# A two-layer attention and MLP kernel: a priority table and new durations for its planner, LayerNorm in tile pairs, PSUM cleared by matmuls, Q and K weights in halves

## The chip, the cores and the metric

One core of one Trainium2 chip. The metric is device time in microseconds (us), the median of several executions. In the profile PE is the engine for matrix multiplication (PEld its weight load), DVE the vector engine, ACT the engine for activation functions, POOL the GpSimd engine, SP the engine that issues the DMA copies. PSUM is the memory that PE writes its results to; an eviction is a copy from there to SBUF, by ACT or DVE. "Granted clock" is the share of full TensorE clock that the records show.

## The reference

A block of sliding-window attention (32 heads of 16, window 256) and an MLP with GELU, both behind a LayerNorm, applied twice to 2048 rows of 512, with the same weights both times.

```python
def _A_ref(x, wqkv, wo):                       # H = 32, Dh = 16, W = 256
    q, k, v = ...                              # x @ wqkv, split by heads
    scores = einsum("bhqd,bhkd->bhqk", q, k) * Dh ** -0.5
    mask = (i - j >= 0) & (i - j < W)
    o = einsum("bhqk,bhkd->bhqd", softmax(where(mask, scores, -1e9)), v)
    return o.reshape(B, S, D) @ wo
def _B_ref(x, w1, b1, w2, b2):                 # D = 512, F = 1792
    return gelu(x @ w1 + b1) @ w2 + b2
x = A_x
x = x + _A_ref(_layernorm(x)); x = x + _B_ref(_layernorm(x))
x = x + _A_ref(_layernorm(x)); x = x + _B_ref(_layernorm(x))
```

## The kernel before

The kernel is a list of operations with a small planner. `add` records an operation: its engine, an assumed duration, what it reads and writes, a priority, perhaps a second engine that could do it ("place"). `run` plays the engines forward in assumed time. Each free engine takes the ready operation with the lowest priority number. The resulting order becomes the engines' queues. The program gives each engine its queue in that order, with semaphore waits for what an operation needs. So a plan made with wrong durations is still correct, but its queues may put an operation that is not ready in front of one that is.

```python
class _Plan:
    OVER = {"pe": 0.0, "act": 105.0, "dve": 82.0, ...}   # engine is free this much before the result
    LAT = {..., "act": {"pe": 57.0, "act": 60.0, "dve": 34.0, ...}, ...}
    def add(self, eng, fn, dur, reads, writes, prio, alloc, free, ..., alt): ...
    def run(self): ...                                    # list scheduling, smallest prio first
# ... cut ...
for h in range(2):                                        # PSUM cleared by DVE
    add("dve", lambda e, B, h=h: e.memset(ps[:, 4*h : 4*h+4, :], 0.0), 2200, ...)
# ... cut: X, then Wqkv in three whole parts, Wo, W1, W2, b2, b1 are loaded by SP ...
def layernorm(tau, layer, dst, dcol, dname, prio):        # one tile of 128 rows
    add("dve", bn_stats ...); add("dve", bn_aggr ...)
    add("pool", veps = var + EPS, 215, ...)               # 128 x 1
    add("pool", rstd = veps ** -0.5, 590, ...)            # 128 x 1
    add("dve", xn = (X - mean) * rstd, 310, ...)
    add("pe", transposes ...); evac(...)                  # xn -> PSUM -> xnT
def visit(g):                                             # 160 visits: 512 score columns, 4 PSUM banks
    add("pe", scores of both halves -> 4 banks)
    for half in 0, 1:                                     # the second is ordered after the first
        add("act", exp of 2 banks -> E, 1025, ...)
# ... mask(u): E *= mask on DVE or POOL; pv(c): probabilities times V, which reads Va and Vs,
#     Vs being V shifted by half a tile, copied Va -> Vs by DMA; outproj; mlp ...
```

The softmax here doesn't subtract the row's maximum and nothing guards it: scores larger than these inputs give would overflow.

Of the kernel before, what the change touches and what calls it, by code (L numbers as in the profile page):

```python
# [6 lines left out]
dt = mybir.dt  # L7
# [159 lines left out]

class _Plan:
# [7 lines left out]
        "act": {"pe": 57.0, "act": 60.0, "dve": 34.0, "pool": 78.0, "sp": 75.0},  # L176
# [7 lines left out]
    def __init__(self, pools):  # L184
        self.nodes = []
        self.lw = {}
        self.lr = {}
        self.pools = pools
        self.affinity = 0.0

    def add(self, eng, fn, dur, reads=(), writes=(), prio=0.0, alloc=None, free=(), after=(), geo=None,
            table=None, dma=False, alt=(), war=(), lock=False):
        i = len(self.nodes)
        deps = set(after)
# [13 lines left out]
        if free and eng == "dve":  # L208
# [4 lines left out]
            alts=((eng, fn, dur, 0.0, lock),) + tuple(alt), done=False,  # L213
# [144 lines left out]
def bass_interleave_layers__sliding_block__dense_activation_gelu__prompt_kernel(  # L358
# [13 lines left out]
    P = 128  # L372
# [30 lines left out]
    GLAG = 26  # L403
# [3 lines left out]
    POOL_M = 1175.0  # L407
# [7 lines left out]
    JOBS = [(0, 2), (2, 2), (4, 4), (8, 4), (12, 4), (16, 4), (20, 4), (24, 4), (28, 2), (30, 2)]  # L415

# [9 lines left out]
    with ExitStack() as kctx:  # L426
        S_ = _Sched(nc, kctx)

        def sb(name, shape, dtype=dt.bfloat16):
# [13 lines left out]
        veps = sb("veps", [P, 2 * NT], dt.float32)  # L443
        mhalf = sb("mhalf", [P, 1], dt.float32)
# [25 lines left out]
        })  # L470
# [3 lines left out]
        add("pool", lambda e, B: e.memset(ident[:], 1.0), 150, writes=["ident"])  # L474
        add("pool", lambda e, B: e.affine_select(
            ident[:], ident[:], [[-1, P]], ALU.is_ge, 0.0, base=0, channel_multiplier=1), 300,
            reads=["ident"], writes=["ident"])
        add("pool", lambda e, B: e.affine_select(
            ident[:], ident[:], [[1, P]], ALU.is_ge, 0.0, base=0, channel_multiplier=-1), 300,
            reads=["ident"], writes=["ident"])  # L480
        add("pool", lambda e, B: e.memset(mhalf[:], -0.5), 100, writes=["mhalf"])
        add("pool", lambda e, B: e.memset(parmask[:], 0.0), 100, writes=["parmask"])
        for par in range(2):
            for i in range(HC):
                add("pool", lambda e, B, i=i, par=par: e.affine_select(
                    parmask[:, par : par + 1], parmask[:, par : par + 1], [[0, 1]], ALU.is_ge,
                    1.0 if i % 2 == par else 0.0, base=Dh * i - 1, channel_multiplier=-1), 190,
                    reads=["parmask"], writes=["parmask"])
        add("pool", lambda e, B: e.memset(mask01[:], 1.0), 150, writes=["mask01"])

        for i, conds in enumerate((((1, 0, -1),), ((1, HK, -1), (0, -HK, 1)))):
            for st, base, cm in conds:
                add("pool", lambda e, B, i=i, st=st, base=base, cm=cm: e.affine_select(
                    mask01[:, i, :], mask01[:, i, :], [[st, HK]], ALU.is_ge, 0.0, base=base, channel_multiplier=cm), 250,
                    reads=["mask01"], writes=["mask01"])
        add("pool", lambda e, B: e.tensor_tensor(out=mask01[:, 0, :], in0=mask01[:, 0, :], in1=mask01[:, 1, :], op=ALU.add), 300,
            reads=["mask01"], writes=["mask01"])
        add("pool", lambda e, B: e.tensor_scalar(
            out=mask01[:, 1, :], in0=mask01[:, 0, :], scalar1=-1.0, scalar2=1.0, op0=ALU.mult, op1=ALU.add), 300,
            reads=["mask01"], writes=["mask01"])  # L500
        add("pool", lambda e, B: e.memset(Va[:, :, :, Dh:VW], 1.0), 600, writes=["V%d" % i for i in range(VR)])

        for h in range(2):
            add("dve", lambda e, B, h=h: e.memset(ps[:, 4 * h : 4 * h + 4, :], 0.0), 2200, writes=["ps:init%d" % h], prio=-200)

        def dma(fn, writes, reads=(), dur=2200.0, prio=0.0, issue=330.0):
            add("sp", fn, dur, reads=reads, writes=writes, prio=prio, dma=True, geo=issue)
# [6 lines left out]
        load_x(0, 2, -100, 3900.0)  # L514
        load_x(2, 2, -99.5, 4700.0)
        for which in range(3):
            dma(lambda e, B, which=which: e.dma_start(
                Wqkv_sb[:, :, which * D : (which + 1) * D],
                A_wqkv[:, which * D : (which + 1) * D].rearrange("(c p) n -> p c n", p=P)),
                ["Wqkv%d" % which], prio=-99 + which, dur=6500.0 + 1700 * which)  # L520
        load_x(4, 4, -96, 11000.0)
        dma(lambda e, B: e.dma_start(Wo_sb[:], A_wo.rearrange("(c p) n -> p c n", p=P)), ["Wo"], prio=-95, dur=6000.0)
        load_x(8, 8, -94, 14000.0)
# [12 lines left out]
        def evac(dst, src, n, reads, writes, prio, free=(), after=(), two=False, kind="", boot=False):  # L536

            return add("dve", lambda e, B: e.tensor_copy(dst(B), src(B)), 410 if two else d_psum(n),
                       reads=reads, writes=writes + ([] if free else reads), prio=prio, free=free, after=after,
                       alt=() if kind not in ACT_OK and not boot else (("act", lambda e, B: e.activation(dst(B), src(B), AF.Copy, scale=1.0), d_act(n), 0.0 if boot else ACT_H, False),))  # L540
# [3 lines left out]
        def layernorm(tau, layer, dst, dcol, dname, prio):  # L544

            t = tau % T
            k = 2 * tau + layer
            s = xn_rr[0] % NXN
            xn_rr[0] += 1
            k6 = xn_rr[0] % 8  # L550
            add("dve", lambda e, B: e.bn_stats(stat6[:, k6, :], X[:, t, :]), 680,  # L551
                reads=["X%d" % t], writes=["st%d" % k6], prio=prio)
            add("dve", lambda e, B: e.bn_aggr(statmv[:, k, :], stat6[:, k6, :]), 150,
                reads=["st%d" % k6], writes=["mv%d" % k], prio=prio)
            add("pool", lambda e, B: e.tensor_scalar(
                out=veps[:, k : k + 1], in0=statmv[:, k, 1:2], scalar1=EPS, scalar2=None, op0=ALU.add), 215,
                reads=["mv%d" % k], writes=["ve%d" % k], prio=prio - 500, lock=True)
            add("pool", lambda e, B: e.tensor_tensor(  # L558
                out=rstd[:, k : k + 1], in0=veps[:, k : k + 1], in1=mhalf[:], op=ALU.pow), 590,
                reads=["ve%d" % k, "mhalf"], writes=["rs%d" % k], prio=prio - 500, lock=True)  # L560
            add("dve", lambda e, B: e.tensor_scalar(  # L561
                out=xn[:, s, :], in0=X[:, t, :], scalar1=statmv[:, k, 0:1], scalar2=rstd[:, k : k + 1],
                op0=ALU.subtract, op1=ALU.mult), 310,
                reads=["X%d" % t, "mv%d" % k, "rs%d" % k], writes=["xn%d" % s], prio=prio, lock=True)
            g = "tp%d" % k

            def tr(e, B):
                for c in range(DC):
# [4 lines left out]
                alloc=("o", [(g, 1)]), geo="f", war=[dname])  # L573
            evac(lambda B: dst[:, :, dcol : dcol + P],
                 lambda B: psb[:, B[g][0], 0 : DC * P].rearrange("p (c q) -> p c q", c=DC), 512,
                 ["ps:" + g], [dname], prio, free=[g], two=True, kind="t", boot=True)

        def pe_group(g, mms, dur, step, reads, prio, cls="o", after=(), fresh=True, war=()):

            for i in range(0, len(mms), step):  # L580
                part = mms[i : i + step]

                def fn(e, B, part=part):
# [6 lines left out]
                    alloc=(cls, [(g, 1)]) if (i == 0 and fresh) else None, geo="f", after=after, war=war)  # L590

        def residual(tau, layer, g, prio):
            t = tau % T
            add("dve", lambda e, B: e.tensor_tensor(out=X[:, t, :], in0=X[:, t, :], in1=ps[:, B[g][0], :], op=ALU.add),  # L594
                d_psum(512), reads=["X%d" % t, "ps:" + g], writes=["X%d" % t], prio=prio, free=[g])

        def lnq(b, prio):

            xs = b % 2
            for j in range(2):  # L600
                layernorm(2 * b + j, 0, xnTA[:, xs], j * P, "xa%d_%d" % (xs, j), prio)
            xr = ["xa%d_0" % xs, "xa%d_1" % xs]
            cols = [b % QR] + ([QR] if b % QR == 0 and b % RB else [])
            for i in range(DC // 2):
# [3 lines left out]
                for n, cb in enumerate(cols):  # L608
# [4 lines left out]
                        free=[g] if n == len(cols) - 1 else (), after=prev, kind="q", boot=b < 2),)  # L613

        def proj(g, which, i, xs, xr, prio, war):
            for half in range(2):
# [3 lines left out]
                         256, 2, xr + ["Wqkv%d" % which], prio, fresh=(half == 0), war=war)  # L620

        def kv(b, prio, vprio):
# [3 lines left out]
            for i in range(DC // 2):  # L626
# [8 lines left out]
                    prio=prio, free=[g])  # L635
            for j in range(2):
# [3 lines left out]
                              dc == 0, dc == DC - 1) for dc in range(DC)], 512, 1, xr + ["Wqkv2"], vprio, war=["V%d" % (tau % VR)])  # L640
                evac(lambda B, tau=tau: Va[:, tau % VR, :, 0:Dh],
                     lambda B, g=g: ps[:, B[g][0], :].rearrange("p (h d) -> p h d", d=Dh), 512,
                     ["ps:" + g], ["V%d" % (tau % VR)], vprio, free=[g], kind="v", boot=b < 1)
# [15 lines left out]
        def attention(b, prio):  # L659
# [11 lines left out]
            def visit(g):  # L671
# [13 lines left out]
                def sc(e, B):  # L685
# [12 lines left out]
                    writes=["ps:" + gA, "ps:" + gB], prio=pv, alloc=("sc", [(gA, 2), (gB, 2)]), geo="r")  # L698
                aft = (gelu_last[0],) if gelu_last[0] is not None else ()
                a = ()  # L700
                for gi, g_ in enumerate((gA, gB)):
                    if gi == 1:
# [4 lines left out]
                        table="exp", after=a + aft),)  # L707
                last_exp[0] = a[0]

            def mask(u, n):  # L710
# [4 lines left out]
                add("dve", lambda e, B: e.tensor_tensor(out=Ew, in0=Ew, in1=Mw, op=ALU.mult), 355 * n,  # L715
                    reads=["E%d%s" % (es, x) for es in ess for x in "ab"] + ["mask01"], writes=["E%dd" % es for es in ess],
                    prio=prio + 10 * u, lock=True,
                    alt=(("pool", lambda e, B: e.tensor_tensor(out=Ew, in0=Ew, in1=Mw, op=ALU.mult), POOL_M * n, POOL_H, True),))  # L718

            def pv(c):  # L720
# [9 lines left out]
                def fn(e, B):  # L730
# [15 lines left out]
                add("pe", fn, 600.0, reads=rd, writes=["ps:" + g], prio=pr, alloc=("od", [(g, 2)]), geo="c", war=["OD%d" % s])  # L746
                add("dve", lambda e, B: e.transpose(OD[:, s, :], ps[:, B[g][0] : B[g][0] + 2, 0 : 2 * P]), 715,  # L747
                    reads=["ps:" + g], writes=["OD%d" % s], prio=pr, free=[g])
                sums = OD[:, s, :].rearrange("p (a k n) -> p a k n", a=2, n=32)
                add("dve", lambda e, B: e.reciprocal(Rc[:, s, :].rearrange("p (a k) -> p a k", a=2), sums[:, :, :, Dh]), 205,  # L750
                    reads=["OD%d" % s], writes=["Rc%d" % s], prio=pr - 800)

                def norm(e, B):
# [4 lines left out]
                add("dve", norm, 360, reads=["OD%d" % s, "Rc%d" % s], writes=["N%d" % s], prio=pr - 700, lock=True,  # L758
                    alt=(("pool", norm, 741, 0.0, True),))
                add("dve", lambda e, B: e.transpose(OT[:, bs, c, :], Nb[:, s, :]), 420,  # L760
                    reads=["N%d" % s], writes=["OT%d_%d" % (bs, c)], prio=pr - 600)
# [14 lines left out]
            for j in range(2):  # L776
                outproj(2 * b + j, pr + 10 * j)

# [129 lines left out]
```

## Time and profile before

Median 537.6 us in three runs (534.4 to 539.3); the profiled run has a span of 535.7 us. First the page's busy times (busy us, share of the span, instructions), then, over 40 equal slices, PE's busy tenths and the granted clock in tenths, and at last the engines of the chain that ended last (followed back from the last instruction, at each step to what released it):

```profile
PE 472.1 (88%) x8944; PEld 254.8 (48%) x8944; DVE 387.3 (72%) x739; ACT 427.4 (80%) x514; POOL 292.4 (55%) x376
...
PE   3886688998979999599999879998999879989997
...
PEclk9997979999979999689999999999999989999999
...
PE 60%; DVE 18%; ACT 18%; issue 2%; POOL 2%; POOLq 0%; DVEq 0%
```

PE has 63.6 us without work and ACT 108. The table of waits (engine, line, tile, what it waited for: us, times, longest) has this pair near its head, among waits of DVE and POOL:

```profile
ACT E L704 <- PE ps L691: 58.1, 46, 4.4
...
PEld ps L691 <- ACT E L704: 33.5, 70, 1.6
```

Exponentials wait for scores, and scores wait for exponentials to free PSUM: neither engine is full, they miss each other. Next is the start, from the timeline (start, length, engine, line, operation):

```profile
1.29 1.76 DVE L504 MEMSET ps<- 128x2048 f32 x1 [1.29 <-PEq L893]
...
3.43 1.76 DVE L504 MEMSET ps<- 128x2048 f32 x1 [0.38 <-issue]
...
5.11 1.22 DVE L551 BATCH_NORM_STATS2 stat<-X 128x6 f32<-128x512 bf16 x2
...
8.31 0.61 PE L569 MATMUL ps<-ident,xn 128*128 128x128 bf16 x4 [8.31 <-DVE xn L561]
...
10.47 3.19 PE L585 MATMUL ps<-xnTA,Wqkv_sb 128*128 128x256 bf16 x16 [0.69 <-ACT xnTA L540]
...
20.64 1.94 ACT L704 ACTIVATE E<-ps 128x1024 bf16<-128x1024 f32 x2
```

### The profile page before, as it was taken

What the parts mean: (1) busy time and instruction counts of PE and PEld (TensorE: products, weight loads), DVE (VectorE), ACT (ScalarE), POOL (GpSimd) and SP (SyncE); (2) the same over time, 40 slices, a digit from 0 to 9 for tenths busy, and PEclk for the clock granted to TensorE, in tenths of its full rate; (3) what the DMA queues carried; (4) which work ended last, traced back from release to release, by engine and by line L of the source; (5) the groups of instructions that cost most, each with busy time, mean ns of one, the idle gap of its engine ahead of it and who ended that gap; (6) DMA issues with size and microseconds to landing.
All of it is one profiled execution on the core that took longest, in us unless ns stands there. A gap on an engine that the chain in (4) does not pass through costs nothing.

```text
span 535.7 us, 19845 instructions
## 1 busy us (share of the span) xinstructions
PE 472.1 (88%) x8944; PEld 254.8 (48%) x8944; DVE 387.3 (72%) x739; ACT 427.4 (80%) x514; POOL 292.4 (55%) x376
## 2 busy tenths in 40 slices
PE   3886688998979999599999879998999879989997
PEld 2543455555544545345444444444544444444563
DVE  5996878496979578775899588884878648793531
ACT  2689779888987988979888988689876888699552
POOL 6576746274684457452588347860585425871410
PEclk9997979999979999689999999999999989999999
DMA  8910001010100001000000011000110001100000
GB/s 277 325 42 23 2 4 23 1 25 1 24 2 13 12 3 23 4 1 22 14 13 3 2 23 23 2 4 6 33 29 21 2 8 39 42 2 4 29 21 29
DMA packets 16020, 15.82 MB, mean 30 GB/s; under 512 B 3264, under 2 KB 15424, under 8 KB 15936
## 3 DMA queue, kind: packets, MB, share of 16 engines
q1 hardware_dynamic: 15936, 14.56, 9.5%
q8 instruction: 70, 1.15, 0.9%
q14 instruction: 14, 0.11, 0.1%
HBM read 8.00 MB, written 2.10 MB: 19 GB/s over the span
## 4 chain that ended last, share of the span: by engine, by line
PE 60%; DVE 18%; ACT 18%; issue 2%; POOL 2%; POOLq 0%; DVEq 0%
PE ps L585 46%; ACT E L704 12%; PE ps L737 6%; PE ps L691 6%; DVE KT L629 3%; DVE xn L561 2%; DVE stat L551 2%; ACT gT L820 2%; DVE E L715 2%; PE ps L569 2%; DVE OD L747 2%; DVE gT L817 1%; ACT L820 1%; DVE X L841 1%; DVE X L594 1%
## 5 line engine op out<-in xcount | busy, mean ns | idle before, releaser
L704 ACT ACTIVATE E<-ps 128x1024 bf16<-128x1024 f32 x320 | 305.5, 1037 | 58.8 <-PE ps L691 58.1
L718 POOL TENSOR_TENSOR E<-E,mask 128x512 bf16<-128x512 bf16 x151 | 177.3, 1182 | 143.4 <-ACT E L704 143.1
L585 PE MATMUL ps<-xnTB,W_sb 128*128 128x512 bf16 (+1 forms) x560 | 116.8, 347 | 5.1 <-ACT gT L829 2.3
L585 PE MATMUL ps<-W_sb,gT 128*128 128x512 bf16 x448 | 114.9, 380 | 0.3 <-DVE X L841 0.3
L715 DVE TENSOR_TENSOR E<-E,mask 128x512 bf16<-128x512 bf16 x105 | 66.0, 632 | 27.0 <-ACT E L704 26.8
L691 PE MATMUL ps<-QT,KT 32*64 32x320 bf16 (+4 forms) x3072 | 70.2, 267 | 14.8 <-ACT E L704 8.5
L585 PE MATMUL ps<-xnTA,Wqkv_sb 128*128 128x256 bf16 x512 | 71.4, 283 | 8.8 <-DVE KT L629 2.7
L585 PEld LDWEIGHTS ps<-xnTB,W_sb 128*128 128x128 bf16 x560 | 51.9, 101 | 49.4 <-issue 3.9
L691 PEld LDWEIGHTS ps<-QT,KT 32*64 32x64 bf16 x3072 | 34.3, 105 | 68.6 <-ACT E L704 33.5
L829 ACT ACTIVATE gT<-ps,b1T 128x512 bf16<-128x512 f32 (+1 forms) x92 | 50.2, 584 | 18.0 <-PE ps L585 17.7
L837 POOL TENSOR_TENSOR Xb<-X,b2all 128x512 f32<-128x512 bf16 x32 | 37.7, 1179 | 44.3 <-DVE X L841 29.8
L585 PEld LDWEIGHTS ps<-W_sb,gT 128*128 128x128 bf16 x448 | 39.9, 98 | 41.6 <-issue 3.6
L585 PEld LDWEIGHTS ps<-xnTA,Wqkv_sb 128*128 128x128 bf16 x512 | 46.6, 101 | 25.3 <-DVE KT L629 4.1
L747 DVE STREAM_TRANSPOSE OD<-ps 128x512 f32<-128x512 f32 x64 | 45.4, 710 | 17.2 <-PE ps L737 15.7
L737 PE MATMUL ps<-E,Va 64*17 64x64 bf16 (+3 forms) x1920 | 51.0, 240 | 5.8 <-ACT E L704 3.0
L737 PEld LDWEIGHTS ps<-E,Va 64*17 64x17 bf16 x1920 | 40.8, 89 | 27.9 <-issue 16.8
L737 PE MATMUL ps<-E,Vs 64*17 64x64 bf16 (+3 forms) x1920 | 51.7, 240 | 0.0
L629 DVE TENSOR_TENSOR KT<-ps,parmask 128x1024 bf16<-128x1024 f32 x32 | 38.4, 1208 | 17.7 <-PE ps L585 17.3
L841 DVE TENSOR_TENSOR X<-Xb,ps 128x512 bf16<-128x512 f32 x32 | 21.8, 681 | 34.1 <-PE ps L585 33.9
L569 PE MATMUL ps<-ident,xn 128*128 128x128 bf16 x256 | 25.9, 230 | 20.3 <-DVE xn L561 9.8
L561 DVE TENSOR_SCALAR xn<-X,statmv,rstd 128x512 bf16<-128x512 bf16 x64 | 41.5, 653 | 2.7 <-POOL rstd L558 2.5
L551 DVE BATCH_NORM_STATS2 stat<-X 128x6 f32<-128x512 bf16 x64 | 42.2, 665 | 0.4
(45 smaller groups left out, 481.7 us busy)
## 6 DMA issues: line engine op xcount, KB each, us to landing
Vs<-Va SPq DMA_DIRECT2D x64, 68.0 KB, 2.0
W_sb<-in_B_w_dram SPq DMA_DIRECT2D x2, 1792.0 KB, 14.8
out_dram<-X SPq DMA_DIRECT2D x16, 128.0 KB, 1.7
Wqkv_sb<-in_A_wqkv_dram SPq DMA_DIRECT2D x3, 512.0 KB, 7.0
X<-in_A_x_dram SPq DMA_DIRECT2D x1, 1024.0 KB, 10.4
X<-in_A_x_dram SPq DMA_DIRECT2D x2, 256.0 KB, 3.0
X<-in_A_x_dram SPq DMA_DIRECT2D x1, 512.0 KB, 8.4
Wo_sb<-in_A_wo_dram SPq DMA_DIRECT2D x1, 512.0 KB, 9.4
```

Of the source, the lines that this page charges most:

```text
L551: add("dve", lambda e, B: e.bn_stats(stat6[:, k6, :], X[:, t, :]), 680, reads=["X%d" % t], writes=["st%d" % k6], prio=prio)
L561: add("dve", lambda e, B: e.tensor_scalar(out=xn[:, s, :], in0=X[:, t, :], scalar1=statmv[:, k, 0:1], scalar2=rstd[:, k : k + 1], op0=ALU. ...
L585: r = e.matmul(ps[:, B[g][0], cols], lhsT, rhs, start=st, stop=sp)
L629: add("dve", lambda e, B, g=g, i=i: e.tensor_tensor(out=KT[:, kb, :, 2 * i : 2 * i + 2, :].rearrange("p a c q -> p a (c q)"), in0=ps[:, B[ ...
L691: x = e.matmul(ps[HK * par : HK * par + HK, bk[r], o : o + n], KT[rows, kb, par, c, m * HK : m * HK + HK], QT[rows, c, q : q + n], start=T ...
L704: a = (add("act", lambda e, B, g_=g_, gi=gi: e.activation(E[:, 2 * gi : 2 * gi + 2, e0 : e0 + 512], ps[:, B[g_][0] : B[g_][0] + 2, :], AF. ...
L715: add("dve", lambda e, B: e.tensor_tensor(out=Ew, in0=Ew, in1=Mw, op=ALU.mult), 355 * n, reads=["E%d%s" % (es, x) for es in ess for x in " ...
L718: alt=(("pool", lambda e, B: e.tensor_tensor(out=Ew, in0=Ew, in1=Mw, op=ALU.mult), POOL_M * n, POOL_H, True),))
L737: x = e.matmul(ps[32 * r : 32 * r + VW, B[g][par], q_lo * HK : q_hi * HK], V[rows, (2 * b + m // 2) % VR, c * HC + 2 * r + par, :], E[rows ...
L747: add("dve", lambda e, B: e.transpose(OD[:, s, :], ps[:, B[g][0] : B[g][0] + 2, 0 : 2 * P]), 715, reads=["ps:" + g], writes=["OD%d" % s], ...
L829: gelu_last[0] = add("act", lambda e, B, g=g, fc=fc: e.activation(gT[:, fc, 0:M], ps[:, B[g][0], 0:M], AF.Gelu_apprx_tanh, bias=b1T[:, fc ...
L837: add("pool", lambda e, B, t=tau % T, xs=xs: e.tensor_tensor(out=Xb[:, xs, :], in0=X[:, t, :], in1=b2all[:], op=ALU.add), 1180, reads=["X% ...
```

## The change

The intent: make the start shorter, make POOL's part of LayerNorm cheaper, and give the planner both better numbers and, per operation, a priority offset. The table holds one row per kind of operation; rows with a star weigh the second engine of the same kind.

```diff
+_TUNE = {
+    "ln": [-1621, -1617, ...], "sc": [47, 33, ...], "ex": [-671, 101, ...], "mk": [...], "mk*": [...],
+    ...                                        # 35 rows, cut
+}
-        "act": {"pe": 57.0, "act": 60.0, "dve": 34.0, "pool": 78.0, "sp": 75.0},
+        "act": {"pe": 57.0, "act": -105.0, "dve": 34.0, "pool": 78.0, "sp": 75.0},
+        if key is not None:                    # in add()
+            j = self.kidx.get(key, -1) + (not more)
+            ...
+                prio += self.tune[key][j]
+            if alt and key + "*" in self.tune:
+                alt = tuple(a[:3] + (a[3] + self.tune[key + "*"][j],) + a[4:] for a in alt)
-        for h in range(2):
-            add("dve", lambda e, B, h=h: e.memset(ps[:, 4 * h : 4 * h + 4, :], 0.0), 2200, ...)
+        add("dve", lambda e, B: e.memset(gT[:, 0, :], 0.0), 210, writes=["g0"], prio=-300)
+        for h in range(NWARM):                 # NWARM = 18
+            bk = h % 8
+            add("pe", lambda e, B, bk=bk: e.matmul(ps[:, bk, :], gT[:, 0, 0:P], gT[:, 0, :], start=True, stop=True), ...)
-        # parity mask: memset and 16 affine_select on POOL
+        # parity mask: one iota on POOL, two tensor_scalar on DVE
+        load_w(0, 0, D // 2, ...); load_w(1, 0, D // 2, ...)          # Q and K weights in halves
+        load_w(0, D // 2, D // 2, ...); load_w(1, D // 2, D // 2, ...); load_w(2, 0, D, ...)
-        # LayerNorm: veps and rstd, one column per tile
+        # LayerNorm: rstd = var + EPS (POOL or DVE), rstd = rstd ** -0.5, two columns per pair of tiles
-        mask 355, normalise 310, probs times V 600, transposes 715 and 420, reciprocal 205, ... # planner's ns
+        mask 415, normalise 395, probs times V 600 or 310, transposes 712 and 433, reciprocal 240, ...
```

## The prediction

> **What bounds the kernel now.** The page of the profiled execution shows a span of 535.7 us, PE busy 472.1 us (88%), ACT 427.4 (80%), DVE 72%, POOL 55%. In the chain that ended last PE holds 60%, DVE 18%, ACT 18%. Busy time by stretch: in 0 to 20 us PE works 9.5 us and ACT 5.5; in 20 to 480 us PE works 411 of 460 and ACT 389; in the last 55.7 us PE works 51.7. So PE idles about 49 us in the middle and 10.5 at the start. In the table of waits exponentials wait 58.1 us for score matmuls, while score weight loads wait 33.5 us for exponentials to free PSUM: the order of work, not one engine's throughput, makes these gaps. The granted clock averages 0.958, with drops to 0.77.
>
> **Start.** DVE clears PSUM twice (1.76 us each, 1.29 to 5.19), so the first statistics start at 5.11. They feed rstd on POOL, whose queue holds 16 parity-mask selects; the first transpose starts at 8.31, the first exponential at 20.64. The first 16 projection matmuls take 3.19 us, later ones 1.91. The Trainium skill, "TensorE: Matmul & The Clock Gate", Part 1, says an idle PE runs at half clock until about 3.4 us of sustained activity; 3.19 against 1.91 agrees roughly. The change puts 18 matmuls (128x512) in the idle stretch before 8 us, which clear PSUM and wake the clock, frees DVE, shortens POOL's list, and splits Q and K loads so first halves land earlier. I estimate 0.9 us from earlier statistics, 1.3 from warm projections, 1 to 2 from shorter queues and loads: 3 to 4 us, all critical.
>
> **LayerNorm in pairs.** On POOL, 64 additions (252 ns) and 64 powers (596 ns), 54 us, become 32 and 32: 26 us less. Little is direct (DVE's normalise waits 2.5 us for rstd). Indirectly: DVE's mask multiply has median 426 ns, mean 632; its normalise 414 and 653. The Trainium skill, "SBUF — State Buffer", describes a port pair that DVE and GpSimd lock for a whole instruction; the bimodal durations agree. Fewer POOL operations block DVE less: estimated 5 us of DVE time, perhaps 1 us of span. Against it, a pair's first tile waits for the second's statistics (0.8 us).
>
> **Priority table.** Same matmuls, exponentials, GELUs; corrected planner durations; offsets reorder all queues and move masks and evictions between DVE, POOL and ACT. This is most of the effect. It can attack PE's 49 us of idle middle and ACT's 58.1 us wait for scores. PE's busy 472 us is a near floor. I estimate that 40 to 50% of the middle idle goes: about 22 us.
>
> **Sum.** 537.6 - 3.5 - 1 - 22 = 511 us; range 497 to 525. Chance of faster by over 2%: 0.90; within 2%: 0.08; slower: 0.02.
>
> **What would show it.** PE busy share rises to about 92% with PE busy nearly unchanged (about 470, with 6 us of warm-up); ACT share to 83%; exponentials' wait for scores from 58 to about 35 us; first transpose near 7 us, first exponential near 16 to 17; first projections near 120 ns each; POOL's rstd groups near 28 us; DVE's mean mask time below 632 ns. Last 50 us unchanged, PE-full.
>
> **What would make it wrong.** If throttling deepens (mean clock below 0.94), the gain shrinks to 2 to 3%. If the order suits only the plan's durations, new waits appear on DVE or POOL. If it frees more than half of PE's idle, the time falls below 500.

## More of the kernel before

The columns are the window, its length, busy time and instruction count of PE, PEld, DVE, ACT and POOL, then the granted clock, DMA share and GB/s:

```profile
215.00:216.00 1.00, 0.72 (x30) 0.55 (x28) 1.00 (x4) 1.00 (x3) 0.50 (x1) 1.00 0.00 0
216.00:217.00 1.00, 0.17 (x4) 0.00 (x0) 1.00 (x3) 1.00 (x2) 0.38 (x2) 1.00 0.06 16
217.00:218.00 1.00, 0.42 (x16) 0.16 (x16) 0.41 (x2) 1.00 (x3) 1.00 (x2) 0.96 0.00 0
218.00:219.00 1.00, 0.76 (x40) 0.72 (x48) 0.00 (x0) 1.00 (x3) 0.68 (x2) 0.50 0.00 0
219.00:220.00 1.00, 0.50 (x47) 0.33 (x24) 0.41 (x1) 1.00 (x3) 0.91 (x1) 0.50 0.00 0
...
230.00:231.00 1.00, 1.00 (x4) 0.30 (x2) 0.26 (x2) 0.37 (x1) 0.56 (x1) 0.50 0.00 0
231.00:232.00 1.00, 1.00 (x4) 0.27 (x2) 0.78 (x2) 0.00 (x0) 1.00 (x2) 0.72 0.00 0
232.00:233.00 1.00, 1.00 (x20) 0.47 (x20) 0.81 (x2) 0.42 (x1) 0.70 (x1) 1.00 0.00 0
```

The slices of 13.4 us show "6" and "8" here, as if the clock had sunk a little. The fine windows show that it is either 1.00 or 0.50 (0.96 and 0.72 are windows in which it changed). In this stretch it halves after some microseconds in which PE is sparsely used, and comes back after dense use. (The Trainium skill, "TensorE: Matmul & The Clock Gate", Part 1, names these two states; this trace agrees.) While it stands at 0.50, the large matmuls follow each other at twice the distance (128x512: 427 ns against 216 in this trace), so "PE busy" grows for the same work; short groups grow less (16 score matmuls: 0.66 us against 0.42).

## The result, and the profile after

490.41 us median (489.27 to 491.21, 4 runs) against 537.04 us before (4 runs): the ratio is 0.9132, with a 95% interval of 0.9085 to 0.918. Ratios are computed as the mean time of one kernel's fast runs over the mean of the other's fast runs of the same rounds, so they are not quite the ratios of the medians quoted. I had predicted 511 (497 to 525): the direction was right, but the gain of 46.6 us was nearly double the 26 predicted.

The same parts of the page after:

```profile
PE 462.3 (94%) x8962; PEld 252.1 (52%) x8962; DVE 397.4 (81%) x771; ACT 416.0 (85%) x498; POOL 265.8 (54%) x281
...
PE   8859689999999999999999999999999999999997
...
PEclk9979969999999999999999999999999999999999
...
PE 70%; ACT 18%; DVE 7%; POOL 1%; DMA 1%; issue 1%; SPq 1%
```

and of the table of waits:

```profile
PEld ps L943 <- ACT E L956: 37.5, 96, 1.0
ACT E L956 <- PE ps L943: 29.2, 43, 2.3
```

PE's idle time (span minus busy) fell from 63.6 to 26.9 us. PE's busy time fell too, by 9.8 us, though 6.3 us of warm-up were added: 16 us fewer for the same matmuls. The slices show why that is possible: after the sixth (73 us) no slice shows a reduced clock, and the mean clock rose from 0.958 to 0.983; the stretches at half clock cover 44.8 us before and 17.1 after.

The start, from the timeline:

```profile
1.24 6.30 PE L735 MATMUL ps<-gT 128*128 128x512 bf16 x18 [1.24 <-DVE gT L732]
...
3.49 1.29 DVE L788 BATCH_NORM_STATS2 stat<-X 128x6 f32<-128x512 bf16 x2 [1.05 <-DMA X<-in_A_x_dram]
...
7.37 0.61 PE L821 MATMUL ps<-ident,xn 128*128 128x128 bf16 x8
...
9.53 1.03 PE L837 MATMUL ps<-xnTA,Wqkv_sb 128*128 128x256 bf16 x8
...
17.08 7.44 ACT L956 ACTIVATE E<-ps 128x1024 bf16<-128x1024 f32 x8 [2.32 <-PE ps L943]
```

The first exponential comes 3.6 us earlier and projections run at 1.03/8 = 129 ns instead of 3.19/16 = 199 ns. That is what I predicted for the start. The clock's record is no help here: it begins at 13.1 us before and at 5.8 us after, and windows without a record read 1.00. The times of the single matmuls tell more. Before, the 128x256 projections follow each other at 213 ns until 13.0 us and then at 109; after, the 128x512 warm-up matmuls do so at 427 ns until 5.5 us and from 5.9 us at 216. So the warm-up ended the slow start some 7 us earlier, and the mean clock leaves that start out. But a little later the changed kernel has this:

```profile
27.81 0.43 PE L943 MATMUL ps<-QT,KT 32*64 32x320 bf16 x24
...
30.59 2.25 POOL L970 TENSOR_TENSOR E<-E,mask 128x512 bf16<-128x512 bf16 x2 [0.26 <-ACT E L956]
32.99 0.39 PE L989 MATMUL ps<-E,Va 64*17 64x256 bf16 x4 [4.75 <-POOL E L970]
```

PE stands idle for 4.75 us, put down to POOL's masks, in front of the first probabilities times V. In the kernel before, the first probabilities times V started at 29.87 with no such gap:

```profile
29.87 0.28 PE L737 MATMUL ps<-E,Va 64*17 64x256 bf16 x4 [0.22 <-issue]
```

### The profile page after: what moved, and what is told of

Read it like the earlier page. It is cut to its first block, busy times and chain, and to the rows that moved or that the text cites. A ratio compares the mean times of both kernels' runs of the same rounds, so it can differ in the third digit from the quotient of the medians.

```text
span 489.2 us, 19785 instructions
## 1 busy us (share of the span) xinstructions
PE 462.3 (94%) x8962; PEld 252.1 (52%) x8962; DVE 397.4 (81%) x771; ACT 416.0 (85%) x498; POOL 265.8 (54%) x281
## 4 chain that ended last, share of the span: by engine, by line
PE 70%; ACT 18%; DVE 7%; POOL 1%; DMA 1%; issue 1%; SPq 1%
PE ps L837 51%; ACT E L956 14%; PE ps L989 8%; PE ps L943 8%; PE ps L821 2%; DVE KT L881 1%; ACT gT L1081 1%; DMA X<-in_A_x_dram 1%; DVE E L967 1%; POOL E L970 1%; DVE stat L788 1%; SPq L747 1%; DVE OD L999 1%; ACT gT L1072 1%; DVE xn L811 1%
## 5 line engine op out<-in xcount | busy, mean ns | idle before, releaser
L956 ACT ACTIVATE E<-ps 128x1024 bf16<-128x1024 f32 x320 | 302.9, 1037 | 32.1 <-PE ps L943 29.2
L970 POOL TENSOR_TENSOR E<-E,mask 128x512 bf16<-128x512 bf16 x142 | 172.1, 1217 | 110.7 <-ACT E L956 110.0
L837 PE MATMUL ps<-W_sb,gT 128*128 128x512 bf16 x448 | 116.7, 381 | 0.1
L837 PE MATMUL ps<-xnTB,W_sb 128*128 128x512 bf16 (+1 forms) x560 | 109.8, 337 | 0.9 <-DVE gT L1069 0.3
L967 DVE TENSOR_TENSOR E<-E,mask 128x512 bf16<-128x512 bf16 x114 | 76.6, 673 | 14.9 <-ACT E L956 14.0
L837 PE MATMUL ps<-xnTA,Wqkv_sb 128*128 128x256 bf16 x512 | 68.7, 277 | 2.6 <-DVE KT L881 1.5
L989 PE MATMUL ps<-E,Va 64*17 64x64 bf16 (+3 forms) x1920 | 49.4, 235 | 7.7 <-POOL E L970 6.5
L989 PE MATMUL ps<-E,Vs 64*17 64x64 bf16 (+3 forms) x1920 | 50.2, 235 | 0.0
L1006 POOL TENSOR_TENSOR Nb<-OD,Rc 128x256 bf16<-128x256 f32 x42 | 28.4, 677 | 23.0 <-DVE Rc L1002 20.8
L989 PEld LDWEIGHTS ps<-E,Vs 64*17 64x17 bf16 x1920 | 40.4, 86 | 0.1
```

Of the source, the lines that this page charges most:

```text
L837: r = e.matmul(ps[:, B[g][0], cols], lhsT, rhs, start=st, stop=sp)
L956: a = (add("act", lambda e, B, g_=g_, gi=gi: e.activation(E[:, 2 * gi : 2 * gi + 2, e0 : e0 + 512], ps[:, B[g_][0] : B[g_][0] + 2, :], AF. ...
L967: add("dve", lambda e, B: e.tensor_tensor(out=Ew, in0=Ew, in1=Mw, op=ALU.mult), 415 * n, reads=["E%d%s" % (es, x) for es in ess for x in " ...
L970: alt=(("pool", lambda e, B: e.tensor_tensor(out=Ew, in0=Ew, in1=Mw, op=ALU.mult), POOL_M * n, POOL_H, True),))
L989: x = e.matmul(ps[32 * r : 32 * r + VW, B[g][par], q_lo * HK : q_hi * HK], V[rows, (2 * b + m // 2) % VR, c * HC + 2 * r + par, :], E[rows ...
L1006: return e.tensor_tensor(out=Nb[:, s, :].rearrange("p (k a d) -> p a k d", a=2, d=Dh), in0=sums[:, :, :, 0:Dh], in1=Rc[:, s, :].rearrange( ...
```

## The experiments

Theory A, formed after the result: nearly all of the gain is the order of the queues, from the planner's numbers and the table together, because PE is idle less often and, being denser, keeps its full clock; the start's gain is real but is lost in the stall at 28 to 33 us. The rivals: the structural parts carry the gain; the clock is a limit of power, so it has nothing to do with the order; the table gains by a better split of work between engines. Where a run says "in its own order", the planner ran exactly as in the changed kernel and only its finished list was edited, so that nothing else moved. Such edits are told in words in the diffs of e2 to e6; the actual code is longer.

| run | median us | ratio to before | 95% interval |
|---|---|---|---|
| changed kernel | 490.4 | 0.9132 | 0.9085 to 0.918 |
| e1_no_table | 523.0 | 0.9747 | 0.9703 to 0.9791 |
| e2_dve_clear | 489.5 | 0.9114 | 0.9079 to 0.9149 |
| e3_unpaired | 491.0 | 0.9147 | 0.9116 to 0.9178 |
| e4_start_undone | 491.3 | 0.9152 | 0.912 to 0.9184 |
| e5_late_w2 | 485.4 | 0.9033 | 0.8989 to 0.9077 |
| e6_late_w2_old_start | 490.3 | 0.9123 | 0.9079 to 0.9166 |
| e7_before_new_durations | 520.7 | 0.9695 | 0.9631 to 0.976 |
| e8_before_scores_twice | 538.0 | 1.0004 | 0.9946 to 1.0062 |
| e9_places_only | 529.4 | 0.9864 | 0.983 to 0.9898 |
| e10_pe_keys | 517.4 | 0.9626 | 0.9595 to 0.9657 |
| e11_other_keys | 528.7 | 0.9856 | 0.9822 to 0.989 |
| e12_late_w2_twice | 485.3 | 0.9045 | 0.9019 to 0.9071 |
| e13_before_act_chain | 520.0 | 0.9696 | 0.9637 to 0.9754 |
| e14_before_other_numbers | 526.3 | 0.9812 | 0.9755 to 0.9869 |
| e15_no_place_offsets | 520.2 | 0.9698 | 0.9631 to 0.9765 |

All gave correct results. The median of before in these rounds was 535.8 to 536.8 us.

### e1: no table

```diff
-        }, _TUNE)
+        }, {})
```

> The changed kernel with an empty table: LayerNorm in pairs, PE clearing, split loads and the corrected planner durations stay, the planner chooses the order with its old priorities. Theory A (the table's order is the gain, the rest is worth about 5 us): 528 to 536 us, clock near 0.96, PE idle in the middle near 45 us. Rival B (the structural parts and corrected durations carry most of the 46 us, the table only polishes): 495 to 512 us.

Measured 523.0 us, between the two expectations. The table is worth 32.6 us; 13 to 14 us remain without it. The clock was already 0.980, which I had expected near 0.96.

### e2: PSUM cleared by DVE again

```diff
-# 18 matmuls of zeros on PE
+# two DVE memsets of 128x2048 at the front of DVE's queue; all other queue entries as in the changed kernel
```

> The changed kernel in exactly its own order (queues frozen), but the 18 PE matmuls are gone and DVE clears PSUM with two memsets as before. Theory A (clearing on PE frees DVE and wakes the clock, all on the critical path at the start): slower by 2 to 4 us, 492 to 494.5, first projection matmuls near 200 ns instead of near 125. Rival B (the start is absorbed later, or bounded by the weights' arrival): slower by less than 1 us.

489.5 us against 490.4: no loss (the intervals overlap). Yet its trace shows the expected delay: the first exponential starts at 19.74 us instead of 17.08, and the first 8 projections took 1.87 us instead of 1.03. By the first probabilities times V (32.78 us here, 32.99 in the changed kernel) these 2.7 us are gone. Rival B was right on the time, so something after the start absorbs it.

### e3: LayerNorm's rstd per tile again

```diff
-rstd[:, k : k+2] by one addition and one power
+rstd[:, k] and rstd[:, k+1] by two additions and two powers, at the same place in the queues
```

> The changed kernel in its own order, but each rstd operation over two tiles is done as two operations over one tile at the same place. Adds about 32 x (0.25 + 0.6) = 27 us on POOL and DVE. Theory A (POOL has slack, pairing is worth about 1 us): 490.5 to 493 us. Rival B (POOL's time and its lock on DVE's port matter): 496 us or more.

491.0 us, 0.6 us above the changed kernel's median, within the spread. The trace shows POOL busy 281.2 us instead of 265.8. POOL had the room. Pairing is worth a microsecond at most, as predicted.

### e4: the whole start undone

```diff
-warm-up matmuls; Q and K weights in halves; parity mask from iota
+DVE memsets; Q and K weights whole; parity mask by 16 POOL selects (all in the changed kernel's own order)
```

> The changed kernel in its own order with the whole start as before: DVE clears PSUM, Q and K weights whole, parity mask by 16 POOL selects; only the order of the body and the pairs stay. Theory A (the start is worth 4 to 6 us): 494 to 497 us, first exponential 3 to 5 us later than in the changed kernel. Rival B (start is worth over 10 us because delays at the start multiply through the frozen order): 501 us or more.

491.3 us: 0.9 us above the changed kernel, not 4 to 6, although its first exponential starts at 21.35, 4.3 us later. The first probabilities times V start at 34.19 here and at 32.99 in the changed kernel, so most of the lead is gone by that point. PE's wait just before it is 1.69 us here, not 4.75, and it is put down to an exponential:

```profile
34.19 0.39 PE L989 MATMUL ps<-E,Va 64*17 64x256 bf16 x4 [1.69 <-ACT E L956]
```

### e5: the second MLP weight and the b2 broadcast loaded later

```diff
 # SP's queue only
-... W1, W2, b2all, b1raw, Vs x52 ...
+... W1, b1raw, Vs x8, W2, b2all, Vs x44 ...
```

> The changed kernel in its own order on PE, DVE, ACT and POOL; only the sync engine's queue differs: the second MLP weight and the b2 broadcast are issued after the first 8 copies of shifted V instead of before them. Theory A (in the changed kernel PE stands idle from 28.2 to 33.0 us because those copies queue behind 1.8 MB of weights, and its clock halves after it; this stall swallows what the start gains): the idle stretch goes, 482 to 487 us. Rival B (the stall is caused by the work before it or is made up later): 489 to 491 us.

485.4 us, 5 us faster than the changed kernel by the medians, and faster than both kernels (its interval ends below the changed kernel's). These lines of e5's timelines settle what PE had waited for:

```profile
29.31 0.28 PE L989 MATMUL ps<-E,Va 64*17 64x256 bf16 x4 [0.83 <-DMA Vs<-Va]
...
30.83 2.26 POOL L970 TENSOR_TENSOR E<-E,mask 128x512 bf16<-128x512 bf16 x2 [0.25 <-ACT E L956]
```

POOL's masks run at the same time as in the changed kernel (30.83 against 30.59), but PE starts at 29.31 without them. So the releaser named in the changed kernel's profile, POOL's mask, only happened to end at about that time. The real wait was for the copies Va to Vs, of which the first probabilities times V need eight. SP's queue shows what stood before them, first in the changed kernel (W2 is L763), then in e5:

```profile
10.45 1.28 SPq L763 DMA_DIRECT2D W_sb<-in_B_w_dram  x1
11.77 7.44 SPq L770 DMA_DIRECT2D b2all<-in_B_b_dram  x1
21.34 21.67 SPq L897 DMA_DIRECT2D Vs<-Va  x10
```

```profile
12.31 15.19 SPq L897 DMA_DIRECT2D Vs<-Va  x8
27.54 0.59 SPq L763 DMA_DIRECT2D W_sb<-in_B_w_dram  x1
28.17 0.96 SPq L770 DMA_DIRECT2D b2all<-in_B_b_dram  x1
```

In the changed kernel W2 landed at 26.09 us, the b2 broadcast at 26.39 and the eight copies from 28.02 to 32.55; the first of them kept SP 4.53 us in issuing and took 6.7 us to land (median 2.0). In e5 the first copy still stood behind W1 and took 10.1 us, but the eighth landed at 28.96. The edit moves W2 (1.8 MB) and the b2 broadcast (SP spent 7.44 us issuing it) together, so their shares are not separated. The Trainium skill, "DMA: Bandwidth & Descriptors", "Queues, rings and completion order", says that each DMA engine consumes descriptors in ring order; the landings in the order of issue agree. The 5 us are not the idle time alone: the half-clock stretch that follows the stall in the changed kernel (29.7 to 36.5 us) is gone too.

### e6: the same with the old start

```diff
 # e5 plus the edits of e4
```

> The run before with the whole start undone as in e4 (DVE clears PSUM, whole loads, parity mask by POOL selects). Theory A (the start's gain was hidden by the stall for shifted V): without the stall the old start costs 3 to 5 us again against late W2 with the new start. Rival B (the start is worth nothing for another reason): equal within 1 us.

490.3 us against 485.4 for e5 in the same rounds: the old start now costs 4.9 us, where it cost 0.9 with the stall. Its first exponential came at 21.16 us against 17.32. Start and place of W2 now make a square of four runs, with these times (us) in their traces:

| start, W2 | median | first exponential | eighth copy to Vs lands | first probabilities times V |
|---|---|---|---|---|
| new, early (changed kernel) | 490.4 | 17.08 | 32.55 | 32.99 |
| old, early (e4) | 491.3 | 21.35 | 33.84 | 34.19 |
| new, late (e5) | 485.4 | 17.32 | 28.96 | 29.31 |
| old, late (e6) | 490.3 | 21.16 | 33.92 | 34.27 |

In all four PE starts 0.35 to 0.44 us after the eighth copy lands, in e4 too, where the profile names an exponential that ended at the same time. This shows how the start's gain was hidden: with W2 in front, the copies do not land earlier when the start does.

### e7: only the planner's numbers

```diff
 # kernel before
-"act": {"pe": 57.0, "act": 60.0, ...}; mask 355; normalise 310; probs times V 600; ...
+"act": {"pe": 57.0, "act": -105.0, ...}; mask 415; normalise 395; probs times V 600 or 310; ...
```

> The kernel before with only the planner's numbers changed as in the change (mask 415, normalise 395, transposes, reciprocal, the pool copies, probability times V 310 where short, exponential after exponential -105, DMA issue 450), no table, no structural part. Theory A (of the 13 us that the changed kernel without table keeps, most come from the planner's better numbers): 522 to 528 us, clock near 0.98. Rival B (they come from the pairs and the start, which shift every later choice): 533 to 539 us.

520.7 us: 16 us less than before, with not one operation changed, only the order and the places. Together with e1 this closes the sum: the numbers give 16.0 us; pairs and start, with the other order that the planner then chooses, cost 2.3 (523.0 against 520.7); the table gives 32.6.

For the kernels whose traces hold all matmuls, the span splits like this (idle is span minus busy; the time lost to the clock is worked out as (1 - mean clock) x span, idle time included; the last column is half of PE's busy time within the half-clock stretches, an estimate of the most that they added to it):

| kernel | span | PE busy | of it warm-up | PE idle | clock | lost to the clock | of it in PE busy |
|---|---|---|---|---|---|---|---|
| before | 535.7 | 472.1 | 0 | 63.6 | 0.958 | 22.5 | 17.1 |
| e7, new numbers | 518.8 | 465.1 | 0 | 53.7 | 0.984 | 8.3 | 8.1 |
| e1, all but the table | 520.1 | 469.4 | 6.2 | 50.7 | 0.980 | 10.4 | 8.3 |
| changed kernel | 489.2 | 462.3 | 6.3 | 26.9 | 0.983 | 8.3 | 5.7 |
| e5 | 484.1 | 460.4 | 5.4 | 23.7 | 0.989 | 5.3 | 3.9 |

The planner's numbers bring the clock back. The table hardly touches the clock: it fills PE's idle time (23.8 of its 30.9 us between these two traces). The other 7.1 us are PE busy time, of which the clock explains at most 2.6; the rest is open.

### e8: more work for PE, in the kernel before

```diff
 # kernel before, in its own order: 31 of 160 score visits, in and before the sparse stretches
-for c, m, q, o, n in pieces:
+for c, m, q, o, n in pieces * (2 if (b, g) in TWICE else 1):
```

> The kernel before in its own order; 31 of the 160 score visits, those in and just before the three long sparse stretches (43 to 55, 58 to 75, 149 to 160, 215 to 232 us), run their matmuls twice: the same values again, about 31 x 0.36 = 11 us more PE work. Theory A (the granted clock falls because PE is sparsely used there, so it is lost time that denser use gives back): mean clock rises from 0.958 to 0.97 or more and the time stays within 3 us of before or falls. Rival B (the clock falls by power or heat, more work lowers it): mean clock at or below 0.955 and 8 to 15 us slower.

The clock rose from 0.958 to 0.977 in the profiled runs and the time stayed (ratio 1.0004), with an estimated 11 us of useless PE work added (31 visits at 0.36 us). The other three runs of e8 had 0.968 to 0.971, the eleven of before in these rounds 0.952 to 0.968 (median 0.962), so the typical rise is about 0.01. Here are three of the four stretches, first before, then with doubled scores (columns as for the windows above):

```profile
58.00:75.00 17.00, 10.87 (x344) 7.05 (x344) 12.28 (x22) 14.68 (x18) 10.87 (x12) 0.80 0.01 3
...
149.00:160.00 11.00, 8.38 (x229) 5.16 (x230) 7.63 (x13) 9.31 (x12) 8.53 (x11) 0.69 0.01 1
...
215.00:232.00 17.00, 11.17 (x342) 6.28 (x340) 11.37 (x24) 15.12 (x18) 8.88 (x10) 0.60 0.01 3
```

```profile
58.00:75.00 17.00, 11.42 (x488) 8.12 (x486) 12.24 (x25) 15.94 (x20) 11.20 (x13) 1.00 0.02 4
...
149.00:160.00 11.00, 8.86 (x332) 5.61 (x335) 9.50 (x17) 9.82 (x13) 8.27 (x8) 1.00 0.01 3
...
215.00:232.00 17.00, 13.53 (x525) 8.62 (x528) 13.13 (x25) 15.63 (x18) 9.18 (x10) 0.80 0.02 4
```

With over 40% more matmuls the clock is whole in the first two stretches, and an exponential more fits into each (16 against 15, 11 against 10). The rival, a clock limited by power or heat, predicted the opposite. At 215 to 232 us the clock came back only in part (0.60 to 0.80), and a stretch at 43 to 55 us stayed slow (0.72 to 0.76): there the doubling was not enough. What the clock costs also shows in the unchanged kernel: the eleven runs of before in these rounds go from 534.04 us at a mean clock of 0.968 to 541.23 at 0.953.

### e9, e10, e11, e15: parts of the table

e9 takes only the places (which engine does what) from the whole table; e10 has only PE's rows; e11 only the rows of the other engines; e15 everything but the starred rows.

```diff
-        }, _TUNE)
+        }, {k: v for k, v in _TUNE.items() if k in PE_ROWS})            # e10; e11: not in; e15: no star; e9 plans twice
```

> The changed kernel, planned twice: the first plan with the whole table fixes on which engine every mask, eviction and normalisation runs; the second plan keeps these places and chooses the order with the old priorities. Theory A (the table's 33 us are mostly the order in time, above all on PE): 515 us or more. Rival B (they are mostly the better split of work between DVE, ACT and POOL): 505 us or less.

> The changed kernel with only the PE rows of the table (transposes, Q, K, V, scores, probability times V, output projection, both MLP layers). Theory A (PE's order is what counts): 495 to 510 us, at least half of the 33 us. Rival B (the rows only work together, the offsets were fitted to each other): 515 us or more, as without a table or worse.

> The changed kernel with only the rows of the table for DVE, ACT and POOL operations. Theory A (PE's order is what counts): 515 us or more. Rival B (fitted to each other): 515 us or more too, and then the PE rows alone decide between them.

> The changed kernel with all rows of the table except the six rows of place offsets (which weigh DVE against ACT or POOL). Theory A (order across all engines is the gain and the places follow from it): 505 us or less. Rival B (every row is fitted to the others, the table has to be whole): 512 us or more, as for the PE rows alone (517).

Against 523.0 without a table: places alone 529.4, PE's rows alone 517.4, the others alone 528.7, all but the place offsets 520.2. No part holds even a fifth of the 33 us, and two make things worse. The rows are fitted to each other. My theory that PE's rows would give half of it fell. What replaced it is argued, not shown: the list planner turns a small change into another order, and only the whole table leads to the order for which it was fitted.

### e12: late W2 and doubled scores from 44 to 60 us

```diff
 # e5, and the 8 visits (1,4) to (2,1) run twice
```

> Late second MLP weight as in e5, and 8 score visits, (1,4) to (2,1), run their matmuls twice to keep PE in use from about 44 to 60 us, before and in the stretch from 55.6 to 65.7 us where the clock stood at 0.50. Theory A (clock follows use, and PE is what that stretch waits for once it is slow): clock 0.99 to 1.0 and 1 to 4 us faster than e5. Rival B (the doubled scores delay the exponentials by as much): within 1 us of e5 or slower.

The clock rose to 1.000 over the profiled run (0.989 in e5; 0.995 to 1.000 against 0.986 to 0.993 in the others), and the time was 485.3 against 485.4: no gain. The half-clock stretch that was left in e5 (55.3 to 65.5 us) is gone; that the added matmuls cost as much as it had is the plain reading, but was not measured apart. Rival B was right on the time: after the large sparse stretches are gone, filling the rest with useless work pays nothing.

### e13, e14: which of the planner's numbers

```diff
 # kernel before; e13:                               e14: all the other numbers of e7, this one kept
-"act": {"pe": 57.0, "act": 60.0, "dve": 34.0, ...}
+"act": {"pe": 57.0, "act": -105.0, "dve": 34.0, ...}
```

> The kernel before with one planner number changed: the delay from one ACT operation to the next that depends on it, 60 to -105 (with 105 taken off each ACT operation's occupation, the old number left a hole of 165 ns in the plan between the two exponentials of every visit). Theory A (the hole made the planner put evictions on ACT between exponentials that do not fit there; this number is the larger part of the 16 us): 521 to 529 us, with about 45 evictions on ACT where before had 60. Rival B (the gain comes from the other numbers): 533 to 539 us.

> The kernel before with all the other new planner numbers (mask 415, normalise 395, probability times V 310 where short, transposes, reciprocal, pool copies, DMA issue) and the old delay of 60 between ACT operations. Theory A (the delay is the larger part): 529 us or more, about 60 evictions on ACT. Rival B: 520 to 526 us.

520.0 us with the one number, 526.3 with all the others, 520.7 with both: 16, 10 and 16 us by these medians, so they do not add up. The one number has a plain meaning. The plan frees ACT 105 ns before a result is there, and had the dependent second exponential of a visit start 60 ns after the result. That left a hole of 165 ns in the plan, in which ACT was free and the second exponential not yet ready, so the planner took an eviction if one was. On the chip they sit like this, in ACT's timeline before:

```profile
82.89 0.60 ACT L540 ACTIVATE Va<-ps 128x512 bf16<-128x512 f32 x1
83.38 1.02 ACT L704 ACTIVATE E<-ps 128x1024 bf16<-128x1024 f32 x1
84.28 0.60 ACT L540 ACTIVATE xnTA<-ps 128x512 bf16<-128x512 bf16 x1
84.76 1.05 ACT L704 ACTIVATE E<-ps 128x1024 bf16<-128x1024 f32 x1
```

Fifty exponentials stand before these, so these two belong to one visit. The second one, and with it the release of two PSUM banks, comes some 0.46 us later: 1.38 us from start to start, against 0.92 where this trace has eight exponentials in a row (7.50 us for eight, the last one 1.03). Counted in the traces, evictions on ACT went from 60 (before) to 43 (e13), and operations between the two exponentials of a visit (those that stand after an odd number of exponentials) from 25 to 12. Alone, this number gives as much as all of them together, as theory A said; added last, to the others (526.3 to 520.7), it gives 5.6 us. And e14 keeps 56 evictions on ACT and 25 such interruptions, and still gains 10 us. What e7, e13 and e14 have in common is the clock (0.984, 0.983, 0.980): all three left the order that had the long sparse stretches. That this is the common cause is argued from these numbers, not shown.

## Why the prediction was wrong

Direction and class were right; the size was not. Point by point:

- "PE's busy 472 us is a near floor." Wrong, and the step that failed. The prediction priced the order as idle time of PE alone; PE's busy time was to stay at about 470 us with 6 us of warm-up. It fell to 462.3, so by 16.1 us without the warm-up. I had seen the drops to 0.77 in the clock and took them for a throttle that might deepen ("mean clock below 0.94"). The fine windows show 0.50, set by sparse use, and e8 shows that denser use takes it away. By the table under e7 the half clock had added at most 17.1 us to PE's busy time, and 5.7 after the change: that is at most 11.4 of the 16.1 us, the rest is open.
- "I estimate that 40 to 50% of the middle idle goes: about 22 us", for table and planner numbers in one. This term of the sum was mis-sized too: PE's idle time in the middle fell from 49.1 us (20 to 480) to 19.7 (20 to 435), so by 29.4 us or 60%. The prediction had named this case: "If it frees more than half of PE's idle, the time falls below 500." By the runs, the planner's numbers give 16.0 us (e7) and the table 32.6 (e1 against the changed kernel), 48.6 us together where 22 stood. I had not costed the corrected numbers at all. I only mentioned them.
- "3 to 4 us, all critical" for the start. The first exponential did come 3.6 us earlier, but "all critical" was wrong: with the start undone (e4) the kernel loses 0.9 us, because in the changed kernel PE waits until 32.99 us for the copies of shifted V behind W2, and with the old start it gets there at 34.19. Without this stall the start is worth 4.9 us (e5 against e6).
- "Perhaps 1 us of span" for the pairs: 0.6 us in e3, within noise. Right. POOL's rstd groups came to 23.3 + 3.9 = 27.2 us against the 28 predicted. But "DVE's mean mask time below 632 ns" was wrong: it rose to 673. What the Trainium skill, "SBUF — State Buffer", says of the lock between DVE and GpSimd fits the durations: before, the 21 masks on DVE beside which POOL did nothing took 376 to 426 ns, the 84 beside a POOL operation 354 to 1393. But after the change 98 of 114 masks overlapped with POOL, so a smaller POOL total did not make DVE wait less. In e3, where only the pairs are undone, the mean mask took 690 ns, and DVE's busy time was 396.2 us against 397.4: the "5 us of DVE time" are not seen.
- Right, or nearly: PE's share rose (to 94%, predicted 92%), exponentials' wait for scores fell (29.2 us, predicted 35), first transpose (7.37, predicted 7), first exponential (17.08, predicted 16 to 17), first projections (129 ns, predicted 120), and the last 54 us unchanged (PE busy 50.7 of 54.2; before 51.7 of 55.7).

What stays open: why this particular order is 30 us better than the planner's own. e9 to e11 and e15 show that no group of rows carries it. How the offsets were found is not told by the kernel.

## What to carry to other kernels

Read the granted clock in windows of a microsecond before calling busy time a floor: on a PE with gaps, part of it may be half-speed time that comes back when the gaps close. Give a list scheduler better durations before any tuning: mending one wrong delay gave 16 us here. Treat a fitted table of offsets as one piece: with any of the three parts that I took out, most of its gain was lost. When work at the start gets faster, look for the next wait that does not move with it, here a DMA, and test it by moving only that DMA; of the versions here, late W2 (485.4 us) is the one to keep.

## What the Trainium skill lacked or had wrong

- "TensorE: Matmul & The Clock Gate", Part 1, lists the half clock as coming after an idle window of about 3.4 us. The length agrees: in the ten traces that hold all matmuls (before, after, e1 to e8), all changes of the clock within a trace fall on a grid of 3.41 us. The condition does not: none of the 31 falls in them followed an idle window. PE was busy for 0.18 to 0.56 of the grid window before a fall (0.53 of 214.5 to 217.9 us in the stretch shown), and for 0.78 to 1.00 of the one before a rise. The same part also tells of a kernel whose clock swings because PE idles briefly between groups of matmuls, but no page says how much use is enough. Nor do these traces quite: some windows with a share of 0.46 to 0.56 passed without a fall, and some of up to 0.81 without a rise. The number of matmuls does not settle it either: in 17 us, 344 left the clock at 0.80, 488 made it 1.00, and 525 in another stretch only 0.80.
- "DMA: Bandwidth & Descriptors" says that descriptors are consumed in ring order, which agrees. It has no number for what a small copy pays behind a large load: here 6.7 us to landing at most against a median of 2.0, with 4.53 us of SP's time for one issue (10.1 and 6.75 us behind W1 in e5). Moving the load and the b2 broadcast behind eight copies gave 5 us of the kernel's time.
- No page that I used warns that a wait for several semaphores may be put down to a releaser that was not the one waited for: the 4.75 us charged to POOL were the DMA's (e5).
